# Another order of products and weight conversions around the first and the last output product of the gated block

## The chip, the cores and the metric

The kernel runs on one core of a Trainium2 chip. The metric is the device time of one execution in microseconds. Before the change three runs gave a median of 984.12 us (981.72 to 986.41).

## The reference, cut to what matters

Three layers follow one another on 4 sequences of 576 tokens. All numbers are float32; the weights come as float64.

```
attention: 8 heads of 64, rotary q and k, softmax, times v        -> x (4, 576, 512)
gated:     h = gelu(x @ w_in); u, v = halves of h (512 columns each)
           v_n = layernorm(v) * g_ln
           v_s[b,t,d] = sum_s w_sg[t,s] v_n[b,s,d] + b_sg[t]
           x = x + (u * v_s) @ w_out
mixer:     y = x + (U V)^T along the tokens                        (rank 32)
           out = y + relu(y @ w_ch1) @ w_ch2                       (512 -> 2048 -> 512)
```

## The kernel before, in words

Precision is made from two parts: a float32 value a is split in a high part (ScalarE copies it to the type fp32r) and a low part (a minus its high part, subtracted on GpSimd). A product of two such values is three matrix products: high by high, high by low, low by high. `mm3` issues them on one PSUM tile; its matmuls are line 551. PSUM has four tiles for all of this (pool `ps2`), so a product can start only when an evacuation has freed a tile.

The attention is written out by hand for every engine (lines 383 to 485). From line 487 on only TensorE's order is the program's order. The order of ScalarE, VectorE, GpSimd and of the DMA queue (SyncE) is made by a planner at build time, which runs a simulated timeline: an instruction that comes earlier in the program goes first among those that are ready, and a later one fills the gaps that the simulated timeline shows. On the chip each engine then works through its list in that fixed order.

For each sequence b the gated block has these steps, of which each `[b, index]` is one PSUM tile:

- `v_step(b, t)`: x times the v half of w_in for 128 tokens (12 matmuls of 512 columns); two of them share a tile. Then gelu (ScalarE), layernorm statistics (VectorE, GpSimd), and the split in VH and VL, which lie in SBUF once and are written again for each sequence. The step reads the sequence's XH and XL and the weights WVH, WVL.
- `u_step(b, k0)`: the u half, transposed, with WUH, WUL; gelu writes `ug` (lines 612 to 619).
- `s_step(b, d)`: the spatial product w_sg by v_n for 128 features (28 matmuls of 288). Its evacuation is a chain over three engines: VectorE scales and adds the bias (line 631) and multiplies by `ug` (line 632), ScalarE copies the high part GH (line 633), GpSimd subtracts the low part GL (line 634, shown as line 515).
- `o_step(b, e)`: w_out by GH and GL (24 matmuls of 288, the parts k = 0 to 3 in order, each with the operands GH, GL, GH), then VectorE adds the result to X[b] (line 643). Each o_step reads all four GH and GL.
- `y_step`, `z_step`, `h_step`: the mixer's product along the tokens: transposes of X[b] with a split in YH and YL, a product with U, the split Z, and a product with V, added to X[b].

Then the channel mixer `c1` (w_ch1, relu, split in RH and RL) and `c2` (w_ch2) run over 4 groups of 512 hidden columns and 5 blocks of 472 tokens (the last 416). Their inputs UH, UL are made by `u_split` (one ScalarE copy, one GpSimd subtraction per sequence touched). For block 0 these lie in the memory of XH and XL, and RH, RL of block 0 in the memory of VH and VL.

Weights come as float64, in chunks of 128 rows by 512: one DMA of 512 KB into a raw tile, one ScalarE operation (line 71), four on VectorE (lines 72 to 75), then the high part on ScalarE (line 704 for `weights`, line 534 for w_out) and the low part on GpSimd (line 515). `weights(p2, 0, ...)` has eight chunks, four of w_ch1 (W1) and four of w_ch2 (W2); each `next(w)` writes one. Their raw tiles are the three buffers `gt`, which gelu of v_step uses too; the converted float32 tile has two buffers. Group 0 is written into the four tiles of SETA, which until then hold w_in: WUH, WUL, WVH, WVL.

Of the kernel before, what the change touches and what calls it, by code (L numbers as in the profile page):

```python
# [52 lines left out]
def tile_kernel(ctx: ExitStack, tc: tile.TileContext, qk, vv, tabs, w_in, g_ln, wsgT, b_sg, w_out, u_r, v_r, w1, w2, out):  # L53
    nc = tc.nc

    def f(ap):
        return ap.bitcast(F32)

    def h2(ap):
        return ap.rearrange("p (a b) -> p a b", a=2)  # L60
# [28 lines left out]
    KT = DM // P  # L89
# [6 lines left out]
    def staged(pool, src, tag="raw64", bufs=2):  # L96

        raw = pool.tile([P, 512, 2], U32, tag=tag, name=tag, bufs=bufs)
        t = pool.tile([P, 512], F32, tag="t64", name="t64", bufs=1 if tag == "raw64" else 2)
        nc.sync.dma_start(raw.rearrange("p n w -> p (n w)"), src)  # L100
        for fn in from_f64(t, raw):
            fn()
        return t
# [3 lines left out]
    SETA = [keep.tile([P, KT, 512], F32R, name=f"setA{i}") for i in range(4)]  # L107
# [384 lines left out]
    p2 = es2.enter_context(tc.tile_pool(name="p2", bufs=1, reuse_waits="tile"))  # L492
    ps2 = ctx.enter_context(tc.tile_pool(name="ps2", bufs=4, space=PSUM, reuse_waits="tile"))

    def ps_tile(name):
        return ps2.tile([P, 2, 512], F32, tag="ps", name=name)
# [17 lines left out]
    def less(out, a, b):  # L514
        return nc.gpsimd.tensor_tensor(out, a, b, ALU.subtract)  # L515
# [29 lines left out]
    def mm3(ps, pairs, halves):  # L545
        n = len(pairs)
        for j, (l, r) in enumerate(pairs):
            for a in range(halves):
                rr = r[:, a * HALF:(a + 1) * HALF] if halves == 2 else r
                o = ps[:, a, :HALF] if halves == 2 else ps  # L550
                nc.tensor.matmul(o, l, rr, start=(j == 0), stop=(j == n - 1))  # L551

    def x_split(b):
        for k in range(KT):
            x_hi(b, k)
            x_lo(b, k)
        if b % 2 == 0:
            x_tail(b)
# [53 lines left out]
    def u_step(b, k0):  # L612
        ps = ps_tile(f"u{b}_{k0}")
        pr = []
        for k in range(KT):
            wh, wl = WUH[:, k, k0 * P:(k0 + 1) * P], WUL[:, k, k0 * P:(k0 + 1) * P]
            pr += [(wh, XH[:, k]), (wh, XL[:, k]), (wl, XH[:, k])]
        mm3(ps, pr, 2)
        nc.scalar.activation(h2(ug[:, k0]), ps[:, :, :HALF], AF.Gelu_apprx_tanh)

    def s_step(b, d):
        ps = ps_tile(f"m{b}_{d}")
        ds_ = slice(d * P, (d + 1) * P)
        pr = []
        for s in range(NC - 1):
            pr += [(VH[:, s, ds_], WSH[:, s]), (VH[:, s, ds_], WSL[:, s]), (VL[:, s, ds_], WSH[:, s])]
        tail = VT[:, ds_] if b % 2 else VH[:, NC - 1, ds_]
        pr += [(tail, WSH[:, NC - 1]), (tail, WSL[:, NC - 1])]
        mm3(ps, pr, 2)
        g = p2.tile([P, S], F32, tag="g", name="g", bufs=2)  # L630
        nc.vector.scalar_tensor_tensor(h2(g), ps[:, :, :HALF], gh[:, d:d + 1], h2(bh), ALU.mult, ALU.add)
        nc.vector.tensor_tensor(g, g, ug[:, d], ALU.mult)
        nc.scalar.activation(GH[:, d], g, AF.Copy)
        less(GL[:, d], g, f(GH[:, d]))
# [14 lines left out]
    def y_step(b, s):  # L649

        pp, nt = TS[s], min(2, NC - s)
        pt = ps_tile(f"t{b}_{s}")
        for j in range(nt):
            for k in range(KT):
                nc.tensor.transpose(pt[:pp, j, k * P:(k + 1) * P], X[b][:, k, (s + j) * P:(s + j) * P + pp], ident)
        YH = p2.tile([P, 2, DM], F32R, tag="YH", name="YH", bufs=2)
        nc.scalar.activation(YH[:pp, :nt], pt[:pp, :nt], AF.Copy)
        if s == NC - 1:
            nc.vector.tensor_tensor(YH[pp:, 0], pt[:pp, 0], f(YH[:pp, 0]), ALU.subtract)
            YS[b, s] = YH[:, 0],  # L660
            return
        YL = p2.tile([P, 2, DM], F32R, tag="YL", name="YL", bufs=2)
        nc.vector.tensor_tensor(YL[:pp, :nt], pt[:pp, :nt], f(YH[:pp, :nt]), ALU.subtract)
        for j in range(nt):
            YS[b, s + j] = YH[:, j], YL[:, j]

    def z_step(b, s):
        if s == 0:
            ZS[b] = ps_tile(f"z{b}")
        pz = ZS[b]  # L670
        u4 = U4[:, s].rearrange("p a r -> p (a r)")
        for j, y in enumerate(YS.pop((b, s))):
            nc.tensor.matmul(pz[:, 0, :], u4, y, start=(s == 0 and j == 0), stop=(s == NC - 1))
        if s == NC - 1:
            Z = p2.tile([P, 2, DM], F32R, tag="YL", name=f"Z{b}", bufs=2)[:, 0]
            nc.scalar.activation(Z, pz[:, 0, :], AF.Copy)
            nc.vector.tensor_tensor(Z[64:128], pz[64:128, 0, :], f(Z[64:128]), ALU.subtract)
            ZS[b] = Z
# [19 lines left out]
    def weights(pool, g, tiles):  # L698

        W[g] = tiles  # L700
        for hi, lo, src in ((tiles[0], tiles[1], w1[:, g * 2 * FG:(g + 1) * 2 * FG]), (tiles[2], tiles[3], w2[g * FG:(g + 1) * FG])):
            for k in range(KT):
                t = staged(pool, src[k * P:(k + 1) * P], *(("gt", 3) if g == 0 else ()))
                nc.scalar.activation(hi[:, k], t, AF.Copy)  # L704
                less(lo[:, k], t, f(hi[:, k]))
                yield

    def spans(blk):

        first = t = sum(WIDE[:blk])  # L710
        end = t + WIDE[blk]
        while t < end:
            b, o = divmod(t, S)
            n = min(end - t, S - o)
            yield b, slice(o, o + n), slice(t - first, t - first + n)
            t += n

    def u_split(blk):
        for b, xs, us in spans(blk):
            x, hi = X[b][:, :, xs], UH[blk][:, :, us]  # L720
            nc.scalar.activation(hi, x, AF.Copy)
            less(UL[blk][:, :, us], x, f(hi))
# [3 lines left out]
    def c1(g, blk, i):  # L726

        if i == 0:
            RS[g, blk] = (
                (flat(VH, FPG * WIDE[0]), flat(VL, FPG * WIDE[0])) if (g, blk) == (0, 0) else  # L730
                [p3.tile([P, FPG, max(WIDE)], F32R, tag=t, name=t, bufs=2)[:, :, :WIDE[blk]] for t in ("RH", "RL")]
            )
        RH, RL = RS[g, blk]
        ps = ps_tile(f"r{g}_{blk}_{i}")
        for a in range(2):
            j = 2 * i + a
            js = slice(j * P, (j + 1) * P)
            pr = []
            for k in range(KT):
                pr += [(W[g][0][:, k, js], UH[blk][:, k]), (W[g][0][:, k, js], UL[blk][:, k]), (W[g][1][:, k, js], UH[blk][:, k])]  # L740
            mm3(ps[:, a, :WIDE[blk]], pr, 1)
        s = slice(2 * i, 2 * i + 2)
        nc.scalar.activation(RH[:, s], ps[:, :, :WIDE[blk]], AF.Relu)  # L743
        nc.vector.scalar_tensor_tensor(RL[:, s], ps[:, :, :WIDE[blk]], 0.0, f(RH[:, s]), ALU.max, ALU.subtract)  # L744
# [20 lines left out]
    def run(fn, b, *which):  # L765
        for x in which:
            fn(b, x)
# [17 lines left out]
    for b in range(B - 1):  # L785
        n = b + 1
        for d in range(KT):
            if d == 1 and n > 1:
                x_split(n)
            s_step(b, d)  # L790
            next(ow, None)
        run(v_step, n, 0, 1)
        run(o_step, b, *range(KT))
        run(v_step, n, 2, 3)
        if n < B - 1:
            run(y_step, b, 0, 2)
            v_step(n, 4)
            us = iter(range(KT))
            if n % 2:
                u_step(n, next(us))  # L800
            run(z_step, b, *range(NC - 1))
            y_step(b, 4)
            u_step(n, next(us))
            z_step(b, 4)
            u_step(n, next(us))
            run(h_step, b, 0, 1)
            u_step(n, next(us))
            run(h_step, b, 2, 3)
            run(u_step, n, *us)
        else:  # L810
            v_step(n, 4)
            run(u_step, n, *range(KT))
    a, b = B - 2, B - 1
    w = weights(p2, 0, SETA)
    for d in range(KT):
        s_step(b, d)
        next(w)
        if d < 2:
            y_step(a, 2 * d)
    u_split(0)  # L820
    run(z_step, a, *range(NC - 1))
    y_step(a, 4)
    for e in range(KT):
        o_step(b, e)
        next(w)
        if e == 0:
            z_step(a, 4)
    run(h_step, a, *range(KT))
    c1(0, 0, 0)
    run(y_step, b, 0, 2)  # L830
    c1(0, 0, 1)
    run(z_step, b, *range(NC - 1))
# [86 lines left out]
```

## Time and profile before

| what | value |
|---|---|
| median of 3 runs | 984.12 us |
| the profiled execution's own time | 985.69 us |
| its span | 983.9 us |
| mean granted TensorE clock | 0.979 |
| TensorE matmul busy | 944.0 us of the span |
| VectorE / ScalarE / GpSimd busy | 512.7 / 343.7 / 376.0 us |

Up to about 324 us the attention runs, the gated block with the mixer's token product from there to about 599 us, the channel mixer from about 572 us to the end. Time is in microseconds from the start of the span. A timeline row is: start, duration, engine, source line, operation, output <- inputs, sizes, count, and in brackets the engine's idle time before it with what ended it. In matmul rows the duration is that of the pipelined group, so the next row starts before it ends; the distance of two starts is what one group costs. A granted clock of 1.00 is 2.4 GHz, 0.50 is 1.2 GHz.

### The profile page before, as it was taken

What the parts mean: (1) busy time and instruction counts of PE and PEld (TensorE: products, weight loads), DVE (VectorE), ACT (ScalarE), POOL (GpSimd) and SP (SyncE); (2) the same over time, 40 slices, a digit from 0 to 9 for tenths busy, and PEclk for the clock granted to TensorE, in tenths of its full rate; (3) what the DMA queues carried; (4) which work ended last, traced back from release to release, by engine and by line L of the source; (5) the groups of instructions that cost most, each with busy time, mean ns of one, the idle gap of its engine ahead of it and who ended that gap; (6) DMA issues with size and microseconds to landing.
All of it is one profiled execution on the core that took longest, in us unless ns stands there. A gap on an engine that the chain in (4) does not pass through costs nothing.

```text
span 983.9 us, 13240 instructions
## 1 busy us (share of the span) xinstructions
PE 944.0 (96%) x5212; PEld 821.2 (83%) x5212; DVE 512.7 (52%) x721; ACT 343.7 (35%) x549; POOL 376.0 (38%) x325
## 2 busy tenths in 40 slices
PE   6899999989999997999999799999999999999998
PEld 3677777767787897999999698899889988899887
DVE  7667776767765385334328836655522551222222
ACT  4366655646556452423214422322210320101010
POOL 7667767867852584332426532212200220000000
PEclk7899999999999998999999799999999999999999
DMA  5577677767751500000002101222200210000112
GB/s 175 142 183 199 168 180 181 188 148 189 187 116 38 159 26 1 1 1 1 23 22 87 43 22 43 86 86 65 86 22 1 65 44 1 1 1 20 59 40 75
DMA packets 58948, 78.00 MB, mean 79 GB/s; under 512 B 31403, under 2 KB 35270, under 8 KB 58886
## 3 DMA queue, kind: packets, MB, share of 16 engines
q1 hardware_dynamic: 58886, 77.16, 28.6%
q8 instruction: 41, 0.67, 0.3%
q14 instruction: 21, 0.17, 0.1%
HBM read 55.02 MB, written 4.79 MB: 61 GB/s over the span
## 4 chain that ended last, share of the span: by engine, by line
PE 79%; DVE 9%; DMA 6%; issue 2%; POOL 1%; SPq 1%; ACT 1%; DVEq 0%; POOLq 0%; ACTq 0%
PE a L551 20%; PE r L551 20%; PE pv L281 10%; PE st L245 6%; PE w L551 5%; PE u L551 4%; PE sm L217 3%; PE v L551 3%; PE m L551 3%; DMA Q<-mt 2%; DVE MX L222 2%; DMA g<-in_wsgT 1%; DVE t L75 1%; DMA raw<-in_qk 1%; DVE t L74 1%
## 5 line engine op out<-in xcount | busy, mean ns | idle before, releaser
L222 DVE TENSOR_REDUCE MX<-sm 128x1 f32<-128x576 f32 (+1 forms) x160 | 119.5, 750 | 73.4 <-PE sm L217 47.1
L281 PE MATMUL pv<-pc,VV 128*65 128x288 f32 x512 | 146.7, 410 | 0.5 <-DVE sums L302 0.5
L245 PE MATMUL st<-Q,K 65*128 65x288 f32 (+3 forms) x640 | 127.1, 320 | 10.4 <-DMA Q<-mt 4.9
L245 PEld LDWEIGHTS st<-Q,K 65*128 65x128 f32 (+3 forms) x640 | 96.6, 180 | 25.0 <-DVE MX L222 6.9
L743 ACT ACTIVATE RH<-r 128x944 fp32r<-128x944 f32 (+1 forms) x38 | 35.7, 939 | 206.7 <-PE r L551 206.6
L248 ACT ACTIVATE pc<-st 128x576 f32<-128x576 f32 x128 | 82.9, 647 | 70.6 <-PE st L245 67.2
L744 DVE SCALAR_TENSOR_TENSOR RL<-r,RH 128x944 fp32r<-128x944 f32 (+1 forms) x38 | 42.4, 1117 | 123.7 <-ACT RH L743 123.5
L551 PE MATMUL a<-RH,setB 128*128 128x472 f32 (+1 forms) x320 | 95.6, 371 | 0.0
L281 PEld LDWEIGHTS pv<-pc,VV 128*65 128x65 f32 x512 | 69.4, 138 | 30.1 <-issue 1.0
L759 DVE TENSOR_TENSOR X<-a,X 128x416 f32<-128x416 f32 (+4 forms) x65 | 46.4, 745 | 89.6 <-PE a L551 89.5
L217 PE MATMUL sm<-K,Q 128*128 128x288 f32 (+1 forms) x320 | 78.6, 330 | 12.6 <-DVE MX L222 6.4
L551 PE MATMUL a<-RH,setA 128*128 128x472 f32 (+1 forms) x288 | 86.1, 370 | 0.0
L551 PE MATMUL r<-UH,setB 128*128 128x472 f32 (+1 forms) x256 | 76.4, 369 | 0.0
L551 PE MATMUL r<-UH,setA 128*128 128x472 f32 (+1 forms) x256 | 76.2, 370 | 0.0
L217 PEld LDWEIGHTS sm<-K,Q 128*128 128x128 f32 (+1 forms) x320 | 52.7, 185 | 21.6 <-DVE MX L222 8.5
L515 POOL TENSOR_TENSOR setB<-t,setB 128x512 fp32r<-128x512 f32 x16 | 20.7, 1294 | 124.4 <-ACT setB L704 60.3
L551 PEld LDWEIGHTS a<-RH,setB 128*128 128x128 f32 x320 | 60.2, 188 | 6.9
L551 PE MATMUL a<-RL,setB 128*128 128x472 f32 (+1 forms) x160 | 59.6, 372 | 0.0
L551 PEld LDWEIGHTS a<-RH,setA 128*128 128x128 f32 x288 | 54.0, 188 | 6.1
L551 PE MATMUL a<-RL,setA 128*128 128x472 f32 (+1 forms) x144 | 53.4, 371 | 0.0
L551 PEld LDWEIGHTS r<-UH,setA 128*128 128x128 f32 x256 | 48.1, 188 | 5.2
L551 PEld LDWEIGHTS r<-UH,setB 128*128 128x128 f32 x256 | 48.0, 188 | 5.2
(172 smaller groups left out, 1962.9 us busy)
## 6 DMA issues: line engine op xcount, KB each, us to landing
raw<-in_qk SPq DMA_DIRECT2D x31, 576.0 KB
Q<-K SPq DMA_DIRECT2D x87, 144.0 KB
raw<-in_w SPq DMA_DIRECT2D x24, 512.0 KB
VV<-in_vv SPq DMA_DIRECT2D x32, 160.0 KB
rb<-rr SPq DMA_DIRECT2D x15, 288.0 KB
K<-K SPq DMA_DIRECT2D x29, 144.0 KB
raw<-in_w_in SPq DMA_DIRECT2D x8, 512.0 KB
gt<-in_w SPq DMA_DIRECT2D x8, 512.0 KB
```

The lines of the kernel that those rows point to most:

```text
L74: lambda: nc.vector.scalar_tensor_tensor(tu, hi, 0xC0000000, tu, ALU.bitwise_and, ALU.bitwise_or),
L75: lambda: nc.vector.scalar_tensor_tensor(tu, lo, 29, tu, ALU.logical_shift_right, ALU.bitwise_or),
L217: nc.tensor.matmul(ps[:TS[t], n, :HALF], Q1[:, t * P:t * P + TS[t]], K1[:, n * HALF:(n + 1) * HALF], start=True, stop=True)
L222: nc.vector.tensor_reduce(MXs[h % 2][:TS[t], t:t + 1], ps[:TS[t], :, :HALF], AX.XY, ALU.max)
L245: nc.tensor.matmul(ps[:kk, n, :HALF], l[:, c * P:c * P + kk], r[:, ns], start=st, stop=not st)
L248: nc.scalar.activation(h2(pc[:kk]), ps[:kk, :, :HALF], AF.Exp, scale=0.125)
L281: nc.tensor.matmul(o, l, r, start=(c == 0 and j == 0), stop=(c == NC - 1 and j == len(pr) - 1))
L515: return nc.gpsimd.tensor_tensor(out, a, b, ALU.subtract)
L551: nc.tensor.matmul(o, l, rr, start=(j == 0), stop=(j == n - 1))
L743: nc.scalar.activation(RH[:, s], ps[:, :, :WIDE[blk]], AF.Relu)
L744: nc.vector.scalar_tensor_tensor(RL[:, s], ps[:, :, :WIDE[blk]], 0.0, f(RH[:, s]), ALU.max, ALU.subtract)
L759: nc.vector.tensor_tensor(X[b][:, e2, xs], ps[:, :n, us], X[b][:, e2, xs], ALU.add)
```

## The change

The diff moves calls in the program; no product, conversion or transfer is added or taken away.

- In the pass b = 0 the products `v_step(1, 2)` and `v_step(1, 3)` stand ahead of the four `o_step(0, e)` and no longer behind them. (`v_step(1, 4)` issues nothing; it is shared with sequence 0.) Passes b = 1 and 2 keep their order.
- `weights` of group 0 starts in pass b = 2, one chunk of W1 behind each `u_step(3, k0)`, no longer behind each `s_step(3, d)`. The tiles of SETA are taken in another order: W1 goes to WVH and WVL, W2 to WUH and WUL. The four W2 chunks stay behind the `o_step(3, e)`.
- `u_split(0)` stands behind `s_step(3, 1)` and no longer behind all four.
- `c1(0, 0, 0)` stands ahead of the four `o_step(3, e)` and no longer behind them and the `h_step(2, d)`.

```
         run(v_step, n, 0, 1)
+        if b == 0:
+            run(v_step, n, 2, 3)
         run(o_step, b, *range(KT))
-        run(v_step, n, 2, 3)
+        if b > 0:
+            run(v_step, n, 2, 3)
...
         else:
             v_step(n, 4)
-            run(u_step, n, *range(KT))
+            w = weights(p2, 0, SETA[2:] + SETA[:2])
+            for k0 in range(KT):
+                u_step(n, k0)
+                next(w)
     a, b = B - 2, B - 1
-    w = weights(p2, 0, SETA)
     for d in range(KT):
         s_step(b, d)
-        next(w)
         if d < 2:
             y_step(a, 2 * d)
-    u_split(0)
+        if d == 1:
+            u_split(0)
     run(z_step, a, *range(NC - 1))
     y_step(a, 4)
+    c1(0, 0, 0)
     for e in range(KT):
         o_step(b, e)
         next(w)
         if e == 0:
             z_step(a, 4)
     run(h_step, a, *range(KT))
-    c1(0, 0, 0)
     run(y_step, b, 0, 2)
     c1(0, 0, 1)
```

## Rows read from the trace of the kernel before

**Rows 1.** The page: busy time of the engines, granted clock in 40 slices.

```profile
PE 944.0 (96%) x5212; PEld 821.2 (83%) x5212; DVE 512.7 (52%) x721; ACT 343.7 (35%) x549; POOL 376.0 (38%) x325
PEclk7899999999999998999999799999999999999999
```

**Rows 2.** Waits of TensorE, 330 to 620 us: waiter, releaser, total, times, longest.

```profile
PE w L551 <- ACT GH L633: 5.1, 4, 1.5
PE w L551 <- POOL GL L515: 4.8, 4, 1.7
PE w L551 <- DVE g L631: 1.4, 1, 1.4
```

**Rows 3.** Windows: stretch, length, busy (instructions) per engine, granted clock, DMA share, GB/s.

```profile
370.59:391.41 20.82, 15.53 (x98) 14.36 (x96) 11.85 (x17) 4.75 (x7) 10.66 (x9) 0.84 0.00 0
391.41:396.85 5.44, 5.44 (x26) 4.46 (x25) 0.76 (x1) 0.00 (x0) 0.00 (x0) 1.00 0.01 3
396.85:398.52 1.67, 1.67 (x18) 1.67 (x16) 0.41 (x1) 1.47 (x2) 0.00 (x0) 1.00 0.00 0
496.70:509.48 12.78, 12.78 (x98) 12.78 (x97) 4.68 (x9) 2.18 (x3) 3.47 (x4) 1.00 0.14 42
546.72:570.16 23.44, 17.45 (x97) 16.19 (x98) 16.13 (x21) 8.58 (x13) 14.99 (x9) 0.78 0.08 23
550.00:552.00 2.00, 0.53 (x2) 0.30 (x2) 2.00 (x5) 1.23 (x2) 0.97 (x1) 1.00 0.01 2
558.71:562.97 4.26, 4.26 (x19) 4.25 (x18) 2.76 (x5) 2.73 (x4) 1.42 (x2) 0.51 0.00 0
572.28:577.41 5.13, 5.13 (x26) 4.46 (x25) 1.50 (x3) 2.22 (x2) 2.44 (x2) 1.00 0.00 0
600.00:984.00 384.00, 379.91 (x1822) 341.51 (x1820) 142.82 (x199) 67.85 (x88) 36.53 (x26) 1.00 0.14 44
```

**Rows 4.** TensorE's timeline in the first output product of sequence 0.

```profile
379.13 0.85 PE L551 MATMUL w<-GL,WOH 128*128 128x288 f32 x2 [1.68 <-POOL GL L515]
```

**Rows 5.** GpSimd's and VectorE's timelines beside it.

```profile
377.14 3.32 POOL L515 TENSOR_TENSOR GL<-g,GH 128x576 fp32r<-128x576 f32 x2
...
391.61 0.76 DVE L643 TENSOR_TENSOR X<-w,X 128x576 f32<-128x576 f32 x1 [2.44 <-PE w L551]
```

**Rows 6.** TensorE's timeline in the first output product of sequence 3.

```profile
548.11 0.53 PE L551 MATMUL w<-GH,WOH 128*128 128x288 f32 x2 [1.39 <-DVE g L631]
...
552.51 0.75 PE L551 MATMUL w<-GL,WOH 128*128 128x288 f32 x2 [0.97 <-POOL GL L515]
...
557.16 0.85 PE L551 MATMUL w<-GL,WOH 128*128 128x288 f32 x2 [1.05 <-POOL GL L515]
```

**Rows 7.** VectorE's timeline, 527 to 555 us.

```profile
527.97 0.81 DVE L72 TENSOR_SCALAR t<-t 128x512 f32<-128x512 f32 x1 [3.50 <-ACT t L71]
...
530.00 4.63 DVE L75 SCALAR_TENSOR_TENSOR t<-gt,t 128x512 uint32<-128x512 uint32 x1
...
536.88 0.75 DVE L632 TENSOR_TENSOR g<-g,ug 128x576 f32<-128x576 f32 x1
...
552.66 1.83 DVE L632 TENSOR_TENSOR g<-g,ug 128x576 f32<-128x576 f32 x1
```

**Rows 8.** GpSimd's timeline, 520 to 557 us.

```profile
520.30 5.32 POOL L515 TENSOR_TENSOR VL<-gt,VH 128x512 fp32r<-128x512 f32 x2 [1.39 <-ACT VH L602]
...
529.69 4.40 POOL L515 TENSOR_TENSOR XL<-X,XH 128x1888 fp32r<-128x1888 f32 x1 [1.20 <-ACT XH L721]
...
541.17 1.47 POOL L515 TENSOR_TENSOR setA<-t,setA 128x512 fp32r<-128x512 f32 x1 [1.30 <-ACT setA L704]
...
555.29 1.82 POOL L515 TENSOR_TENSOR GL<-g,GH 128x576 fp32r<-128x576 f32 x1 [1.41 <-ACT GH L633]
```

**Rows 9.** TensorE's timeline, where the first spatial product of sequence 3 reads VL.

```profile
530.60 0.43 PE L551 MATMUL m<-WSH,VL 128*128 128x288 f32 x2
```

**Rows 10.** SyncE's timeline, 340 to 570 us: the loads of the eight chunks.

```profile
468.17 79.23 SPq L100 DMA_DIRECT2D gt<-in_w  x8
```

More of the change, by code (lines that the diff above doesn't have):

```diff
@@ L792, in tile_kernel @@
         run(v_step, n, 0, 1)
+        if b == 0:
+            run(v_step, n, 2, 3)
         run(o_step, b, *range(KT))
-        run(v_step, n, 2, 3)
+        if b > 0:
+            run(v_step, n, 2, 3)
         if n < B - 1:
@@ L811, in tile_kernel @@
             v_step(n, 4)
-            run(u_step, n, *range(KT))
+            w = weights(p2, 0, SETA[2:] + SETA[:2])
+            for k0 in range(KT):
+                u_step(n, k0)
+                next(w)
     a, b = B - 2, B - 1
-    w = weights(p2, 0, SETA)
     for d in range(KT):
         s_step(b, d)
-        next(w)
         if d < 2:
             y_step(a, 2 * d)
-    u_split(0)
+        if d == 1:
+            u_split(0)
     run(z_step, a, *range(NC - 1))
     y_step(a, 4)
+    c1(0, 0, 0)
     for e in range(KT):
@@ L828, in tile_kernel @@
     run(h_step, a, *range(KT))
-    c1(0, 0, 0)
     run(y_step, b, 0, 2)
```

## The prediction

> **What bounds the kernel now.** I read the page first: TensorE is busy 96% of the span and VectorE 52%, and the line of the granted clock dips in the slices of the first output products [rows 1]. So a gain has to come from TensorE's own idle time or its clock. Next the waits of TensorE over the gated block: 5.1 + 4.8 + 1.4 = 11.3 us, all at the output product w, for GH, GL and one PSUM tile (the wait named g) [rows 2]. Then the windows, which price idle and clock together. The undisturbed four o_steps, of sequence 1, take 12.78 us, 3.19 each, 0.266 per operand pair; those of sequence 0 take 20.82 at a mean granted clock of 0.84, those of sequence 3 with one z_step inside 23.44 at 0.78 [rows 3]. A z_step's matmuls start 0.24 apart by my reading of the timeline, so the losses are 20.82 - 12.78 = 8.04 us and 23.44 - 12.78 - 0.24 = 10.42 us. Nothing else in the diff's stretch has a wait. Behind 600 us TensorE is busy 379.91 of 384.00 at clock 1.00 [rows 3], so what is gained ahead reaches the end.
>
> Why the operands are late: the g, GH, GL chain runs beside weight conversions, and VectorE works through its list with hardly a gap: a conversion that takes 4.63 us holds it from 530.00, long as the GpSimd subtraction of 4.40 us beside it [rows 7, 8].
>
> **First place (sequence 0).** The planner's lists ahead of this point see the same instructions, so I leave the chain where it is: GL(2) and GL(3) are one GpSimd stretch, 377.14 + 3.32 = 380.46 [rows 5], and TensorE could take GL(2) at 379.13 [rows 4]. Two v_steps (5.44 us [rows 3]) move ahead of the o_steps. They need only XH, XL and weights that the two v_steps before them read too, and a PSUM tile that an earlier g released.
>
> o_step 0 then starts at 370.59 + 5.44 = 376.03. k = 0 and 1: six pairs, 1.60, to 377.63. GH(2) pair to 377.89; wait 1.24 to 379.13; two pairs to 379.66; GH(3) pair to 379.93; wait about 0.6 for GL(3) at 380.5; two pairs to 381.0. Three o_steps of 3.19: 390.6. So the three later products end 0.8 earlier than in the trace (391.41), with the v_steps already done.
>
> What is late next: y_step(0, 0) now follows the last o_step directly and transposes X[0], which VectorE must add first. In the trace that addition starts at 391.61 and takes 0.76, ending 0.96 behind the start of the next product [rows 5]. Three of the first four transposes (1.67/16 = 0.104 each [rows 3]) need other features, 0.31; stall 0.65. The transposes end at 390.6 + 0.65 + 1.67 = 392.9, before at 398.52: **gain 5.6 us**. Gelu and layernorm of the moved steps go beside the o_steps, where ScalarE has 4.75 busy of 20.82 and VectorE 11.85 [rows 3]; without that room they stood in the splits of y_step, as before. Bounds: if the chain came early, o_steps end at 388.8, gain 7.3; if the clock falls again as in the trace, the loss beyond the idle 5.3 us (the sum of the four waits in this product) was 8.04 - 5.3 = 2.7, gain 2.9.
>
> **Second place (sequence 3).** Three edits act together. c1(0, 0, 0), 5.13 us [rows 3], goes ahead of the o_steps and is cover for the chain. It needs W1 and UL: the fourth W1 chunk's low part ends at 541.17 + 1.47 = 542.64, UL (named XL) at 529.69 + 4.40 = 534.09 [rows 8]; TensorE arrives at 546.72. So it costs nothing, and without 4.1 us of this cover it would hold every o_step.
>
> Low end, the chain as in the trace. c1 takes over the wait of 1.39 for the PSUM tile, so it starts at 548.11 [rows 6] and ends at 553.24. o_step 0: k = 0 to 2, nine pairs, 2.39, to 555.63; GH(3) pair to 555.9; GL(3) is done at 555.29 + 1.82 = 557.11 and used at 557.16 [rows 6, 8], wait 1.26; two pairs to 557.7. z 0.24 and three o_steps 9.58: 567.5. In the trace 570.16, and c1's 5.13 still to come: gain 2.66 + 5.13 = 7.8. High end, no wait at all: the whole 10.42.
>
> The W1 conversions move into the u_steps, with tiles free from the last v_step on. In the trace two chunks were converted by then and held by u_steps still reading WUH, and VectorE stood idle 3.50 us up to 527.97 [rows 7]. That idle time can be used, which brings the list behind it forward by 0 to 3.5 us; GpSimd allows less, its VL subtractions run to 525.62 [rows 8]. The chain is at least 1.4 us too late at the low end, so I take the middle, **gain 9.1 us**. The four W1 chunks are 4 loads, 8 ScalarE, 16 VectorE and 4 GpSimd operations, and W2 the same; their loads use the same three buffers on a DMA queue that carries only these eight from 468 to 547 us [rows 10], so no load passes another. c1's relu and split (0.96 on ScalarE and 1.14 on VectorE by the timeline) come behind the chain's last steps, and RH, RL lie in VH, VL, which the s_steps have finished with. y_step(3, 0) loses the cover of c1 but keeps four h_steps (2.1 us) against the 0.96 that X's addition needs: nothing.
>
> u_split(0) I cost at nothing: though it is written last, its GpSimd half already runs at 529.69 [rows 8], as soon as XH is free. The row beside it, 4.63 against 4.40, shows that the two engines hold each other up, and line 632 takes 1.83 against 0.75 us in another place [rows 7]. The Trainium skill says the same (SBUF — State Buffer, "Who interferes with whom"): a VectorE instruction with two SBUF inputs and a GpSimd instruction that reads SBUF exclude each other, and the second one to issue blocks until the first is finished. By that rule a u_split that really moved back beside line 632 would delay the chain, which is rival A.
>
> **Sum.** 5.6 + 9.1 = 14.7 us. The profiled execution's own time is 985.69, giving 971.0; it lies 1.6 above the median of the three runs, from which the sum gives 969.4. I say 970.
>
> **Rivals.**
> A. The chain gets later and the clock falls again. Place: the list of VectorE between 530 and 555 us is planned anew, and the 4.40 us subtraction falls beside a line 632 of a late s_step, or W2 chunks fill what W1 leaves. Each of the gaps is planned on a simulated timeline, which put these conversions ahead of g before too. Price: GL(3) 4.4 later, so 7.8 - 4.4 = 3.4 at the second place with 5.6 at the first gives 9.0: 976.7 from the profiled time. A falling clock alone costs what it cost: 2.7 at the first place, and 10.42 less waits of 5.98 = 4.4 at the second. Against it: with waits of 1.39 and 1.05 in four microseconds the clock was still 1.00 in 550 to 552 us [rows 3], and only fell behind the third wait; 0.5 came back to 1.00 near 562.5 [rows 3].
> B. Slower: the W1 chunks go ahead of layernorm and VL of sequence 3. s_step(3, 0) reads VL(3) at 530.60 [rows 9], and it is done at 520.30 + 5.32 = 525.62 [rows 8]: a slack of 5.0 us. One chunk is 2.2 us of VectorE alone (0.41, 0.41, 0.69, 0.69), 6.6 beside a long subtraction; four are 8.8 to 26. Beyond 5.0 each microsecond stops TensorE, the clock falls (4.4), and from a delay of 5.0 + 14.7 - 4.4 = 15.3 on the kernel is slower; at 26 it is 985.7 - 14.7 + 21 + 4.4 = 996. Against it: v_step stands earlier in the program and two chunks beside it did no harm in the trace.
> C. The change doesn't do what it says: the planner had chunks in the gaps already, c1 is held by a later W1 chunk, and the wait moves from w to r. Then the first place alone gains, 2.9 to 5.6, and the second's waits return: 980 to 983.
>
> **How the numbers follow.** Forecast 0.68 (966 to 974), A 0.19 (974 to 979), C 0.08, B 0.05. The best case is both high ends, 7.3 + 10.4 from the median: 966.4, and 964 with the scatter of the three runs (981.72 is 2.4 below the median). The upper end reaches through A to the edge of C: 980. About 0.5% (4.9 us) is what a measurement of this kernel can tell from no change, so faster means below 979.2. Faster: the forecast, and all but 0.03 of A: 0.84. Same: that 0.03, C and a part of B, 0.12. Slower: B from its deciding point on, 0.04.
>
> **What would show it.** Right: v of sequence 1 in one run of four ahead of the first w; in w of sequence 0 two waits for GL of about 1.2 and 0.6 us and no low clock; one wait under 1 us for X ahead of the transposes; r<-XH ahead of w of sequence 3, with at most one wait of 1.4 ahead of r and one of 1.3 inside w, and clock 1.00 there. Wrong: w of either place still over 16 us; an r that waits for setA or XL; an m of sequence 3 that waits for VL; setA copies later than 540.46 for the fourth W1 chunk.

## The result and the profile after

The changed kernel takes 974.12 us (median of 4 runs, 972.05 to 976.05), the kernel before 984.46 beside it: a ratio of 0.989, interval 0.9863 to 0.9918. Timed a second time on another occasion it took 973.4 (6 runs) against 984.94: 0.9871, interval 0.9842 to 0.9899. The gain is 10.3 and 11.5 us where the forecast's sum was 14.7. The profiled execution took 976.05 us, the longest of the four, and its span is 974.0.

The page of the changed kernel, busy engines and granted clock in 40 slices, beside [rows 1]: TensorE's busy time fell by 5.5 us for the same products (its matmuls run longer at the lower clock), and the two dips of the clock line are gone.

```profile
PE 938.5 (96%) x5211; PEld 817.4 (84%) x5212; DVE 515.3 (53%) x721; ACT 343.6 (35%) x549; POOL 377.1 (39%) x325
PEclk8999999999999999999999999999999999999999
```

TensorE's waits of the changed kernel between 330 and 620 us, beside [rows 2]: the 5.1 us for GH and the 1.4 for g ahead of w are gone, GL fell from 4.8 to 1.6. In their place stand waits that the kernel before did not have. Two are short, 0.5 us each, for X and YH. The others are 2.5 us of an output product for VL<-r (the low part of c1's relu, line 744), and 1.1 us of a spatial product m, called a middle product below, for g: it is the third of sequence 3, and it needs the PSUM tile that g of the first one frees.

```profile
PE w L551 <- DVE VL L744: 2.5, 1, 2.5
PE w L551 <- POOL GL L515: 1.6, 3, 0.9
PE m L551 <- DVE g L631: 1.1, 1, 1.1
PE t L655 <- DVE X L643: 0.5, 1, 0.5
PE z L673 <- DVE YH L659: 0.5, 1, 0.5
```

Where they stand, in TensorE's timeline of the changed kernel (the first three rows sequence 0, the others sequence 3; beside [rows 4, 6]):

```profile
378.62 0.53 PE L551 MATMUL w<-GL,WOH 128*128 128x288 f32 x2 [0.94 <-POOL GL L515]
...
380.02 0.53 PE L551 MATMUL w<-GL,WOH 128*128 128x288 f32 x2 [0.34 <-POOL GL L515]
...
391.27 1.64 PE L655 MATMUL t<-ident,X 128*128 128x128 f32 x13 [0.52 <-DVE X L643]
...
532.21 0.53 PE L551 MATMUL m<-WSH,VH 128*128 128x288 f32 x2 [1.06 <-DVE g L631]
...
550.24 0.54 PE L551 MATMUL w<-GL,WOH 128*128 128x288 f32 x2 [0.27 <-POOL GL L515]
...
557.70 0.62 PE L551 MATMUL w<-GH,WOH 128*128 128x288 f32 x2 [2.50 <-DVE VL L744]
```

Windows of the changed kernel, beside [rows 3] (length, busy per engine, granted clock): the four output products of sequence 0 take 14.58 us at clock 1.00 (before 20.82 at 0.84); those of sequence 3 with their z_step 18.54 at 0.91 (before 23.44 at 0.78). The third window begins at the end of the wait for VL<-r: behind it the clock is 0.54, near its lower level of 1.2 GHz, for 3.75 us.

```profile
375.68:390.26 14.58, 13.30 (x98) 12.83 (x97) 8.57 (x17) 5.16 (x8) 10.62 (x11) 1.00 0.01 1
...
547.16:565.70 18.54, 15.31 (x99) 14.55 (x98) 11.58 (x14) 6.87 (x10) 10.54 (x7) 0.91 0.00 1
557.70:561.45 3.75, 3.75 (x16) 3.75 (x17) 2.06 (x3) 1.80 (x2) 3.51 (x2) 0.54 0.02 4
```

The two spans differ by 9.9 us, and it can be split at instructions that both traces have. The first place, from the first v of sequence 1 to the first u (before 365.10 to 398.52, after 364.75 to 392.67), shrank from 33.42 to 27.92: 5.50. The start of that place came 0.35 earlier. The second place, from the first m of sequence 3 to the first r of c1(0, 0, 1) (before 527.70 to 579.08, after 521.84 to 569.48), shrank from 51.38 to 47.64: 3.74. Behind it 404.82 became 404.52. The second place is what fell short: 3.74 for 9.1.

The cause of the wait for VL<-r is in ScalarE's and VectorE's timelines of the changed kernel (the first and the second group of rows). The last matmul of c1(0, 0, 0) was issued by 547.16. Its relu, VH<-r, ran at 555.53, directly behind the high part of the last W2 chunk (setA), for whose input ScalarE had stood idle 3.59 us:

```profile
554.99 0.63 ACT L704 ACTIVATE setA<-t 128x512 fp32r<-128x512 f32 x1 [3.59 <-DVE t L75]
555.53 0.94 ACT L743 ACTIVATE VH<-r 128x944 fp32r<-128x944 f32 x1
```

```profile
526.79 4.64 DVE L75 SCALAR_TENSOR_TENSOR t<-gt,t 128x512 uint32<-128x512 uint32 x1
531.35 0.81 DVE L631 SCALAR_TENSOR_TENSOR g<-m,gh,bh 128x576 f32<-128x576 f32 x1
...
556.50 1.14 DVE L744 SCALAR_TENSOR_TENSOR VL<-r,VH 128x944 fp32r<-128x944 f32 x1 [1.54 <-ACT VH L743]
```

So ScalarE, idle for 3.59 us of that time, held a finished product back for 8 us, because its list has the conversions first; the product's PSUM tile stayed taken until 557.64 (556.50 + 1.14), and the third output product needed that tile. The Trainium skill (PSUM — Partial Sum Buffer, "Engine vs sequencer instructions") calls the queues of these engines strict FIFO, and the rows agree.

The first row of VectorE is the cause of the wait in the middle product: a conversion of 4.64 us beside GpSimd's subtraction for UL (named XL) holds g of the first middle product until 531.35, 9.51 us behind the first m (before 7.2). That subtraction starts 4.54 us behind the first m, where it started 1.99 behind it before (529.69 [rows 8] and 527.70). The reason is again ScalarE's list: the copy XH, which the subtraction reads, stands behind a W1 conversion that waited 2.24 us for its load (ScalarE's rows, then GpSimd's):

```profile
523.96 0.67 ACT L71 ACTIVATE t<-gt 128x512 f32<-128x512 f32 x1 [2.24 <-DMA gt<-in_w]
524.53 1.77 ACT L721 ACTIVATE XH<-X 128x1888 fp32r<-128x1888 f32 x1
...
526.38 4.50 POOL L515 TENSOR_TENSOR XL<-X,XH 128x1888 fp32r<-128x1888 f32 x1 [4.12 <-ACT XH L721]
```

### The profile page after: what moved, and what is told of

Same layout as the page of the kernel before. It is cut to its first block, busy times and chain, and to the rows that moved or that the text cites. A ratio compares the mean times of both kernels' runs of the same rounds, so it can differ in the third digit from the quotient of the medians.

```text
span 974.0 us, 13234 instructions
## 1 busy us (share of the span) xinstructions
PE 938.5 (96%) x5211; PEld 817.4 (84%) x5212; DVE 515.3 (53%) x721; ACT 343.6 (35%) x549; POOL 377.1 (39%) x325
## 4 chain that ended last, share of the span: by engine, by line
PE 76%; DVE 11%; DMA 5%; issue 3%; POOL 1%; SPq 1%; ACT 1%; DVEq 0%; ACTq 0%; POOLq 0%
PE a L551 21%; PE r L551 20%; PE pv L281 11%; PE st L245 6%; PE w L551 5%; PE sm L217 3%; PE m L551 3%; PE u L551 3%; PE v L551 3%; DVE MX L222 2%; DVE t L75 1%; DVE t L74 1%; DMA raw<-in_qk 1%; DMA g<-in_wsgT 1%; DVE t L72 1%
```

## The experiments

As the start of the second place varies from execution to execution, the length of that place is the finer measure for edits in it; it is given beside each time. What lies behind it took 404.5 to 405.0 us in all traces but one (405.6 in `relu_four_and_pieces`).

**Each place alone.** `only_first` keeps the edit of sequence 0 and takes the other three back:

```
         run(v_step, n, 0, 1)
+        if b == 0:
+            run(v_step, n, 2, 3)
         run(o_step, b, *range(KT))
```

> Only the edit of the pass b = 0 (the two v_steps ahead of the output products), everything at the last place as in the kernel before. Theory (the two places are independent, each gains what its stretch of the trace shows): 5.5 us faster than before, about 979; waits of TensorE for GL of about 0.9 and 0.3 us and for X of 0.5 us in sequence 0, and again 11 us lost (six us of waits, then the low clock) at the output products of sequence 3. Rival (the first place only shifts the loss and the gain comes from the last place): within 1.5 us of before.

Measured: 979.42 us against 985.57, ratio 0.9942 (0.9915 to 0.997): 5.7 us at the first place, as forecast. In its trace the first place takes 28.07 us and the second 50.91, against 33.42 and 51.38 before. `only_last` has the opposite, v_step(1, 2) and v_step(1, 3) behind the output products again, and the edits of sequence 3:

```
-        if b == 0:
-            run(v_step, n, 2, 3)
         run(o_step, b, *range(KT))
-        if b > 0:
-            run(v_step, n, 2, 3)
+        run(v_step, n, 2, 3)
```

> Only the edits around the last sequence (weights in the u_steps, u_split, c1 ahead of the output products), the pass b = 0 as before. Theory (independent places): 3.7 us faster than before by the stretch of the trace, about 980.7, with the wait of 2.5 us for RL (named VL) inside w of sequence 3 and a low clock behind it. Rival (the places are not independent, or the last one gains the 9.1 us of the prediction): below 977.

Measured: 981.7, ratio 0.9969 (0.994 to 0.9998): 3.1 us. Its second place is 46.18 us long, and the wait for VL<-r stands there as in the changed kernel. The low clock that was expected behind it did not come (1.00, see the last section):

```profile
559.58 0.54 PE L551 MATMUL w<-GH,WOH 128*128 128x288 f32 x2 [2.50 <-DVE VL L744]
```

The two gains add up to 8.8 us; with intervals of 2.7 and 2.9 us on either side that agrees with the whole. The shortfall lies in the second place.

**Which edit of the second place.** `c1_moved_weights_not` leaves c1 ahead of the output products and puts W1's conversions back behind the scores (the s_steps of sequence 3):

```
-            w = weights(p2, 0, SETA[2:] + SETA[:2])
-            for k0 in range(KT):
-                u_step(n, k0)
-                next(w)
+            run(u_step, n, *range(KT))
     a, b = B - 2, B - 1
+    w = weights(p2, 0, SETA)
     for d in range(KT):
         s_step(b, d)
+        next(w)
```

> The changed kernel with the weights of group 0 back behind the s_steps, and W1 in WUH, WUL again; c1 stays ahead of the output products. Theory (it is c1 as cover that gains; the conversions come too late in either order, and relu of c1 stands behind the last two high parts of W2 on ScalarE in both): within 1.5 us of the changed kernel, GL of the last s_step within 2 us of where it was before relative to the first s_step, and again a wait of over 2 us for RL inside w. Rival (moving the conversions is what gains): at least 3 us slower than the changed kernel.

Measured: 972.57, ratio 0.9878 (0.983 to 0.9925), as fast as the changed kernel; the second place is 45.59 us. TensorE's timeline shows the 1.39 us that the prediction's low end had put ahead of r, and the wait for the late relu again, 1.65 us where over 2 were expected:

```profile
544.53 0.48 PE L551 MATMUL r<-XH,setA 128*128 128x472 f32 x1 [1.39 <-DVE g L631]
...
553.62 0.52 PE L551 MATMUL w<-GL,WOH 128*128 128x288 f32 x2 [1.04 <-POOL GL L515]
...
559.48 0.54 PE L551 MATMUL w<-GH,WOH 128*128 128x288 f32 x2 [1.65 <-DVE VL L744]
```

`weights_moved_c1_not` is the opposite: W1's conversions in the u_steps, c1 behind the output products and h_steps.

```
-    c1(0, 0, 0)
     for e in range(KT):
...
     run(h_step, a, *range(KT))
+    c1(0, 0, 0)
     run(y_step, b, 0, 2)
```

> The changed kernel with c1(0, 0, 0) back behind the h_steps; the weights stay in the u_steps. Theory (c1 as cover is what gains): GL of the last s_step is done 8.3 us behind the end of the last transposes, as in the changed kernel, so w of sequence 3 waits about 5 us again and the clock falls: 2.5 to 3.5 us slower than the changed kernel. No wait for RL inside w. Rival (moving the conversions is what gains): within 1 us of the changed kernel, or faster since the wait for RL is gone.

Measured: 978.24, ratio 0.9938 (0.9908 to 0.9967), about 4 us slower than the changed kernel; its second place is 49.62 us. TensorE's waits show the output products waiting for GL and GH again, and the wait for g in a middle product, which thus comes with the moved conversions:

```profile
PE w L551 <- POOL GL L515: 2.7, 4, 1.0
PE w L551 <- ACT GH L633: 2.5, 2, 2.0
PE m L551 <- DVE g L631: 1.1, 1, 1.1
```

From the first m to the end of GL(3) it is 29.41 us before, 29.45 with c1 alone moved, and 28.35 in the changed kernel. So the moved conversions bring the end of the chain forward by 1.1 us and lose 1.1 in the middle product. With W1 in its old place the subtraction for UL starts 1.99 us behind the first m, as before (526.11 and 524.12 in `c1_moved_weights_not`), and the middle product does not wait. By the length of the place the moved conversions gain 1.3 us without c1 (50.91 to 49.62) and lose 0.6 to 2.1 with it (45.59 to 46.18 or 47.64, two traces of the changed kernel); the times resolve neither. c1 as cover, work for TensorE while the chain ends, is what gains: 5.3 us by itself (50.91 to 45.59).

**The relu.** `relu_ahead_of_two` tells the planner to issue the third and fourth W2 chunk's conversions behind the relu of c1(0, 0, 0):

```
+    RELU = [None]
...
-        nc.scalar.activation(RH[:, s], ps[:, :, :WIDE[blk]], AF.Relu)
+        RELU[0] = nc.scalar.activation(RH[:, s], ps[:, :, :WIDE[blk]], AF.Relu)
...
     c1(0, 0, 0)
+    RELU0 = RELU[0]
     for e in range(KT):
         o_step(b, e)
-        next(w)
+        with tc.issue_after(RELU0.ins) if e >= 2 else ExitStack():
+            next(w)
```

> The changed kernel, with one order added: on ScalarE the third and fourth chunk of W2 stand behind relu of c1(0, 0, 0), which frees that product's PSUM tile. Theory (relu waits on ScalarE behind the last two high parts of W2, which wait for VectorE, and the third output product of sequence 3 waits for the tile): no wait for RL inside w, clock 1.00 there; the 2.5 us of the wait and the 1.7 us of low clock are gone: 4.2 us faster than the changed kernel, about 970. Rival (the wait named RL is another thing, such as the tile of z or VectorE's list being full): the wait stays over 1.5 us and the time within 1.5 us of the changed kernel.

Measured: 970.89 (968.73 to 973.31), ratio 0.9859 (0.9809 to 0.9909); the second place is 41.97 us. TensorE's waits of this kernel have no VL any more:

```profile
PE m L551 <- DVE g L631: 1.1, 1, 1.1
PE w L551 <- POOL GL L515: 1.1, 2, 0.8
PE t L655 <- DVE X L643: 0.5, 1, 0.5
```

ScalarE runs the relu 25.7 us behind the first m of sequence 3, where it was 33.7, and the output products with z take 13.16 us at clock 1.00 (the ideal by [rows 3] is 12.78 + 0.24):

```profile
548.74 0.94 ACT L744 ACTIVATE VH<-r 128x944 fp32r<-128x944 f32 x1
```

```profile
548.44:561.60 13.16, 13.16 (x101) 13.12 (x100) 8.73 (x15) 6.75 (x10) 7.09 (x6) 1.00 0.01 2
```

The relu's place in ScalarE's list is the cause of the wait, and so of the low clock that followed it in the first trace. The edit holds back VectorE's and GpSimd's work on the two chunks as well, but in the changed kernel VectorE had stood idle 1.54 us for ScalarE ahead of the relu's low part (row at 556.50), so it was not VectorE's list that held it. The place gains 9.41 us over the kernel before, against the 9.1 forecast; the 1.01 to the high end of 10.42 are about the wait of the middle product, which is still there (1.13).

`relu_ahead_of_four` holds all four W2 chunks back (`e >= 0` in place of `e >= 2`).

> The same with all four chunks of W2 behind relu of c1(0, 0, 0), so that none of them lies beside the last three s_steps. Theory (the W2 conversions in the gaps of VectorE are also what makes GL late): GL of the last s_step is done within 5 us of the end of that s_step (in the changed kernel about 11 us), no wait for GL or YH in sequence 3; 5.0 us faster than the changed kernel, about 969. Rival (it is GpSimd's long subtraction or the order of VectorE that makes GL late): GL comes as late as before. Second rival: the fourth chunk of W2 is then late for c2(0, 0, 0), which waits for setA.

Measured: 978.69, ratio 0.9939 (0.9915 to 0.9964), about 5 us slower than the changed kernel where 5 faster were expected; the second place is 50.34 us. The chain is early: GL(3) ends 22.58 us behind the first m, 5.8 earlier than in the changed kernel, which shows that W2's conversions in the gaps had made it late. But the work held back falls due together. In VectorE's timeline two conversions ahead of the last addition to X (line 643) take 3.78 and 2.42 us, beside GpSimd's 7.28 us of UL, and TensorE waits for that addition:

```profile
558.41 3.78 DVE L75 SCALAR_TENSOR_TENSOR t<-gt,t 128x512 uint32<-128x512 uint32 x1
562.12 2.42 DVE L74 SCALAR_TENSOR_TENSOR t<-gt,t 128x512 uint32<-128x512 uint32 x1
564.46 0.75 DVE L643 TENSOR_TENSOR X<-w,X 128x576 f32<-128x576 f32 x1
```

```profile
556.71 7.28 POOL L515 TENSOR_TENSOR UL<-X,UH 128x416 fp32r<-128x416 f32 x3 [1.69 <-ACT UH L721]
```

```profile
565.26 0.85 PE L551 MATMUL q<-VH,Z 128*128 128x288 f32 x2 [6.00 <-DVE X L643]
```

**The wait of the middle product.** `relu_four_and_pieces` adds to that kernel u_split of block 0 in four pieces, so that no conversion is held for more than one piece:

```
-            x, hi = X[b][:, :, xs], UH[blk][:, :, us]
-            nc.scalar.activation(hi, x, AF.Copy)
-            less(UL[blk][:, :, us], x, f(hi))
+            for k in range(KT) if blk == 0 else (slice(None),):
+                x, hi = X[b][:, k, xs], UH[blk][:, k, us]
+                nc.scalar.activation(hi, x, AF.Copy)
+                less(UL[blk][:, k, us], x, f(hi))
```

> The same as relu_ahead_of_four, and u_split(0) in four pieces of one feature block each, so that GpSimd's subtraction of 4.4 us is four of 1.1 us. Theory (the 4.6 us of a conversion on VectorE at the first s_step of sequence 3 are the long subtraction beside it, and the wait of 1.1 us of the third s_step for its PSUM tile follows from it): no VectorE conversion over 2.5 us there, and no wait for g; 1 us faster than relu_ahead_of_four. Rival: a conversion is then held by each piece in turn, and the wait stays.

Measured: 978.17, ratio 0.9935 (0.9902 to 0.9968), no better; the second place is 50.41 us. VectorE now loses a little in five operations in a row, the pieces take 5.92 us together, and the middle product still waits 1.0:

```profile
521.07 1.31 DVE L73 TENSOR_SCALAR t<-t 128x512 uint32<-128x512 uint32 x1
522.41 1.58 DVE L74 SCALAR_TENSOR_TENSOR t<-gt,t 128x512 uint32<-128x512 uint32 x1
524.03 1.59 DVE L75 SCALAR_TENSOR_TENSOR t<-gt,t 128x512 uint32<-128x512 uint32 x1
```

`relu2_sub_vector` is relu_ahead_of_two with that subtraction on VectorE itself:

```
-            less(UL[blk][:, :, us], x, f(hi))
+            if blk == 0:
+                nc.vector.tensor_tensor(UL[blk][:, :, us], x, f(hi), ALU.subtract)
+            else:
+                less(UL[blk][:, :, us], x, f(hi))
```

> The relu ahead of two conversions, and the low part of the first block's UL (the subtraction that writes the tile called XL) taken by VectorE instead of GpSimd. Theory: the 4.64 us of a VectorE conversion beside the 4.50 us subtraction are the two engines holding each other up; with the subtraction on VectorE (estimate 2 to 2.5 us by its size against that of the 0.69 us conversions), the conversion takes 0.69 again, g of the first middle product comes 1 to 2 us earlier, the second middle product no longer waits 1.1 us, and the time falls by 1 to 1.5 us from relu_ahead_of_two. Rival: 4.6 us is that conversion's own time or VectorE's list grows by as much as it wins; the wait of the middle product stays at 1 us or more and the time stays within 0.5 us or rises.

Measured: 970.1, ratio 0.9848 (0.9818 to 0.9878). The subtraction takes 2.12 us on VectorE, where it took 4.50 on GpSimd, and the conversion behind it 1.79 instead of 4.64 (a setA subtraction of 2.51 us runs beside it on GpSimd):

```profile
527.68 2.12 DVE L723 TENSOR_TENSOR XL<-X,XH 128x1888 fp32r<-128x1888 f32 x1
529.72 1.79 DVE L75 SCALAR_TENSOR_TENSOR t<-gt,t 128x512 uint32<-128x512 uint32 x1
```

The middle product's wait falls to 0.34 us and the second place to 41.17, 0.8 us less, so the hold-up is shown as the cause of that wait; its share of the time is below what the runs can tell.

`relu2_weights_back` is relu_ahead_of_two with W1's conversions back behind the scores (the diff of c1_moved_weights_not).

> The relu of c1(0, 0, 0) ahead of the third and fourth W2 conversions, and the W1 conversions put back into the scores' steps. Theory: moving the W1 conversions gained nothing by itself, so this runs within 1.5 us of relu_ahead_of_two (970.9 to a before of 983.5), with no wait for VL<-r in the output products; a wait of about 1.4 for g ahead of r returns, and stands on c1 instead of the output products. Rival: the moved conversions bring the chain forward, which the late relu had hidden; then GL and GH waits of over 1.5 us come back in the output products of sequence 3, the clock falls, and it takes over 973.

Measured: 970.31, ratio 0.9848 (0.982 to 0.9877); the second place is 42.20. The 1.38 us ahead of r come back in place of the 1.13 in the middle product:

```profile
540.53 0.48 PE L551 MATMUL r<-XH,setA 128*128 128x472 f32 x1 [1.38 <-DVE g L631]
```

`relu2_both` has both of these edits.

> The relu ahead of two conversions, the subtraction on VectorE and the W1 conversions back in the scores' steps. Theory: as the kernel with the subtraction on VectorE, within 1 us, for the moved conversions gain nothing. Rival: without the hold-up the place of the conversions decides whether VectorE reaches g in time, and this kernel waits over 1 us more in the middle or output products of sequence 3 than the one with the conversions moved.

Measured: 970.81, ratio 0.9853 (0.9827 to 0.9878). Here the second place has no wait at all, 40.55 us in a window where TensorE is busy throughout, the least seen:

```profile
523.97:564.52 40.55, 40.55 (x295) 39.46 (x294) 33.20 (x46) 18.95 (x27) 21.61 (x14) 1.00 0.18 61
```

The time does not resolve it from the three others with the early relu (970.1 to 970.9).

**The first place.** `one_v_each_side` puts one v_step ahead of the output products of sequence 0 and the other behind them:

```
         if b == 0:
-            run(v_step, n, 2, 3)
+            v_step(n, 2)
         run(o_step, b, *range(KT))
+        if b == 0:
+            v_step(n, 3)
```

> The changed kernel with v_step(1, 2) ahead of the output products of sequence 0 and v_step(1, 3) behind them again. Theory (the end of the output products of sequence 0 is set by GL of its last s_step, not by TensorE's work): the first output product ends where it did, the v_step behind it costs its 2.7 us and saves the wait of 0.5 us for X: u_step(1, 0) starts 2.2 us later (392.7 to 394.9 by the changed kernel's trace), more if the clock falls in the longer waits for GL. Rival (TensorE's own work sets the end): u_step(1, 0) starts 0.5 us earlier.

Measured: 977.0, ratio 0.9917 (0.989 to 0.9943). From the first v to the first u it takes 31.36 us against 27.92, 3.4 more where 2.2 were expected. With 2.7 us less cover the chain stops TensorE again:

```profile
377.24 0.53 PE L551 MATMUL w<-GH,WOH 128*128 128x288 f32 x2 [0.60 <-ACT GH L633]
379.78 0.53 PE L551 MATMUL w<-GL,WOH 128*128 128x288 f32 x2 [2.01 <-POOL GL L515]
```

**The changed kernel again**, on the chip of the three relu2 variants.

> The changed kernel itself, beside the three variants that follow, so that a difference of 3 us between two ratios is read from one chip. Theory: its ratio to the kernel before comes out at 0.988 to 0.991, the third output product of sequence 3 waits 2.5 us for VL<-r again, and the second middle product 1.0 to 1.1. Rival: the 10 us hang on the runs shown, and the ratio lies outside 0.986 to 0.992.

Measured: 973.4, ratio 0.9871 (0.9842 to 0.9899), with waits of 2.3 us for VL<-r and 1.3 in the middle product. All ten runs of the changed kernel have a mean of 973.4, the 22 of the four kernels with the early relu 970.9: these beat both kernels, by 2.6 us against the changed one (two standard errors are 1.5, from the scatter of the runs). On the one chip that ran the changed kernel beside three of the four it is 2.2, with two standard errors of 2.1. The traces promise more, 46.18 or 47.64 against 40.55 to 42.20 at the second place; why the times show less stays open. The stretch ahead of that place ended between 519.3 and 524.1 us in the eleven traces with the whole first edit. The scatter comes from the attention, which no edit touches: from the first v of sequence 1 to the first m of sequence 3 it is 156.6 to 157.4 us in all eleven, while the first v of the block, right behind the attention, starts between 320.7 and 326.0. What makes the attention vary is not known.

## Why the prediction came out as it did

1. First place, 5.6 us: 5.50 measured, and each step as put. With the 0.35 of the earlier start taken out, the output products ended at 390.61 (forecast 390.6). The two waits for GL were 0.94 and 0.34 (1.24 and 0.6), the one for X 0.52 (0.65), the clock 1.00. The transposes ended at 393.02 (392.9).
2. Second place, 9.1 us: 3.74 in the first trace, 5.20 in that of `changed_again` (51.38 to 46.18). The step that failed is "c1's relu and split (...) come behind the chain's last steps", at no cost. They came behind the W2 chunks as well, and c1's PSUM tile was held for it. The term is two prices in the window of the output products, which lost 5.52 us (18.54 against 12.78 + 0.24 = 13.02): 2.50 of this wait, 0.47 and 0.27 of two short ones for YH and GL, and 2.29 that TensorE was busy beyond 13.02 (15.31), most of it for the clock. The wait stands in both traces, the low clock in the first alone. With the relu ahead of two chunks both are gone: 47.64 or 46.18 became 41.97. The prediction had also said what would show it wrong, the output products w of either place still over 16 us, and here they took 18.54: by that sign its second place was wrong.
3. In the same sum, "That idle time can be used, which brings the list behind it forward": GL(3) came 1.06 us earlier and the middle product lost 1.06 to it. In time the edit of the weights can't be told from nothing. The wait for g moved, neither to r nor to w, but to m, and no rival had that: the moved conversions stand ahead of XH in ScalarE's list and delay the subtraction that holds VectorE.
4. c1 as cover: it took the whole lateness of the chain, as reckoned; r waited for nothing, and GL cost 0.27 us inside w (1.26 at the low end).
5. u_split(0) at nothing: right for the move of the call. With that call in its old place every engine's list is the same in the built program; no run was made of it. But its GpSimd half did move, by 2.55 us against the first m (1.99 to 4.54), through the edit of the weights, as said in 3.
6. y_step(3, 0) without the cover of c1: right, no wait there.
7. The rivals: A's falling clock came, but from a wait that A did not name, and the chain itself was not later. B did not come: VL of sequence 3 was never waited for. C did not come either, r waited for nothing; it is the kernel with the weights left alone that has its wait ahead of r.

The total lies inside the forecast's own range of 966 to 974 by the repeat and 0.1 us above it by the first timing, and far inside the whole range, 964 to 980. One term of two was right, in size and in its steps; the other was two to three fifths short, and that the total still falls within the range is owed to its width and is no sign that the second term was understood.

Two sums of the prediction are slightly off: the high end of the first place is 7.4 and not 7.3 (398.52 - 388.81 - 0.65 - 1.67), and where it says that without 4.1 us of cover c1 would hold every o_step, the 4.1 is the time by which W1 is ready ahead of TensorE (546.72 - 542.64).

## What to carry to other kernels

When a product is moved ahead as cover, its evacuation is part of the move: look up what stands ahead of it in the evacuating engine's list and until when it holds the PSUM tile that a later product needs. Weight conversions that fill gaps are harmless only where nothing urgent stands behind them in the same list, and holding all of them back only moves the crowd to the next place. For an edit of a few microseconds the length of its own stretch in the trace decides sooner than the time of the whole run, but not from one trace alone: the same kernel had 47.64 and 46.18.

## What the runs showed of the hardware

- The same wait had two prices. In the first trace of the changed kernel the 2.50 us for VL<-r were followed by 3.75 us at clock 0.54. In that of `only_last` 2.50 us for the same tile were followed by full clock, and so were the 2.35 us in that of `changed_again`, where the second place was 46.18 us instead of 47.64. What decides between the two was not found; the length of the wait alone does not. The windows behind the wait in `only_last` and in `changed_again`:

```profile
559.58:563.50 3.92, 3.92 (x30) 3.92 (x31) 2.54 (x4) 1.81 (x2) 3.69 (x2) 1.00 0.02 4
...
556.11:559.90 3.79, 3.79 (x28) 3.79 (x29) 2.37 (x4) 1.80 (x2) 3.56 (x2) 1.00 0.02 4
```

- The hold-up between VectorE and GpSimd also strikes VectorE operations with one SBUF input: line 73, 0.43 us when undisturbed, took 1.31 beside the pieces of the subtraction (row above). The Trainium skill (SBUF — State Buffer, "Who interferes with whom") has it that tensor_scalar, too, can enter modes that use the port shared with GpSimd, with which the row agrees. The same subtraction is 2.12 us on VectorE and 4.50 on GpSimd.
